# A transformer block in one kernel: a gate tile moves from the attention's filler to the seven-product stage, and the steps around it are set anew

## The chip, the cores and the metric

The kernel runs on one NeuronCore of a Trainium2 chip. The metric is the device time of one execution in microseconds (us); less is better. Engines are named as in the profile: PE (TensorE's matmuls; PEld, its weight loads), DVE (VectorE), ACT (ScalarE), POOL (GpSimd), SP (SyncE, which issues most DMAs).

## The reference

With S = 2048 tokens, width D = 640, 32 heads of 20, a window of W = 256 and a gated layer of Df = 1728:

```python
xn = layernorm(x)
q, k, v = heads(xn @ wqkv)
scores = einsum("bhqd,bhkd->bhqk", q, k) * 20 ** -0.5
mask = (i - j >= 0) & (i - j < 256)
A = einsum("bhqk,bhkd->bhqd", softmax(where(mask, scores, -1e9)), v) @ wo
B = (gelu_tanh(xn @ w_gate) * (xn @ w_up)) @ w_down
return x + A + B
```

Everything is float32. gelu_tanh(g) is 0.5 g (1 + tanh(sqrt(2/pi) (g + 0.044715 g^3))).

## The kernel before

**Precision.** A float32 operand is split into a rounded high part and a low part; a product is three matmuls, high x high, low x high, high x low (`dense_steps`, L104 is its matmul). With 640 = 5 x 128 rows one product of a 128-column weight tile with a chunk of C = 512 tokens is 15 matmuls of 512 columns. There are NC = 4 chunks.

**Stages.** First the layer norm and the first q, k and v products. Then the attention, in units: unit u is a group of four heads (g = u // 4) and a chunk (c = u % 4), 32 in all. Then the pair stage (`gate_up_pair`, matmuls at L893): gate and up products of a tile f for two chunks together, seven products by sums of weights and of tokens in place of eight. Then the output products with `w_down` and `wo` (L1160).

**A unit of attention** has NS = 14 slots, numbered on in `now[0]`. In it lie:
- `max_pair` (matmul L468, DVE L472): scores of 128 queries for two heads, and their masked maximum on DVE; 8 a unit, two at slots 0, 4 and 8 and, from the second unit on, two more at slot 0 behind `av_unit`. They run ahead of the unit that uses them. Their PSUM pool has four banks.
- `exp_piece` (matmul L527, ACT L529): scores and exponentials of one head in one of three banks, two pieces at each of the slots 0, 2, ... 10. The banks are X, Y, Z of `pieces`: X is the diagonal block and the block two back, Y two blocks ahead in the chunk, Z the block one back and one ahead. X and Z read the k of the chunk before. Their PSUM pool (`psx`) has two banks.
- `clear` (POOL L540 and L543) sets masked parts of a finished bank of P to zero, one slot after its last exponential: three clears for X and Y, two for Z (in a first chunk two, three and one).
- `av_unit` (matmul L554) of the unit before, at slot 0; its output takes a bank of `psx` too, which ACT empties (L558).
- `load_stack(u + 3)` at slot 12: twelve DMAs from DRAM on SP's queue, six for q into one of three buffers, six for k into one of four (L447).

**Filler.** Between these, `pull_fill(RATE / NS)` at the end of every slot draws matmuls from a generator, `filler`, which runs the remaining q, k and v products and the gate tiles of `sets`; a matmul counts 1, one of v 0.65. `RATE` is the number a unit. What the attention doesn't draw runs after it. `NFA` is the number of gate tiles in the filler (besides the last, half-wide one): tiles NFA to 12 go to the pair stage. `V1_SLOT` is the slot from which v's second half may be drawn.

**A gate tile in the filler** (`gate_up_fill`) has for each chunk a gate and an up product, each in one of two PSUM banks (`ps_d`), and then five steps on other engines:

```python
c1: gs = copy(gate); t = square(sqrt(0.044715) * gate)      # ACT
c2: t = (t + 1) * gs                                       # DVE L607
c3: t = tanh(sqrt(2 / pi) * t)                             # ACT, LAG slots later
c4: gs = (t + 1) * gs                                      # DVE L615
c5: t = (gs * 0.5) * up                                    # DVE L622, then stored
```

`c5` alone reads the up product, and waits until `c4` has been issued.

**Order.** The order on PE, ACT, DVE and POOL is that in which the Python code issues the instructions. `defer(n, ...)` issues a step n slots later at the slot's start; `late` puts a DVE step behind the maxes and exponentials of its slot (`flush`). `save_qk` uses the same for q and k: a high copy, a difference, and after LAG slots a low copy and a second difference on POOL, then stores.

Of the kernel before, what the change touches and what calls it, by code (L numbers as in the profile page):

```python
# [12 lines left out]
AF = mybir.ActivationFunctionType  # L13
OP = mybir.AluOpType
# [14 lines left out]
SR = 3 * DH  # L29
QROWS = 64 + SR  # L30
NS = 14
RATE = 42.2
V1_SLOT = 158
MXD = 6
LAG = 4
NFA = 6
HD = D // 2
HR = 5
NQD = 9
# [25 lines left out]
def block_kernel(ctx, tc, x, wqk, wv, wgu, wdo, wdl, out):  # L65
    nc = tc.nc
# [17 lines left out]
    qd = [dram.tile([NG, 3, 4 * DH, C], BF, name=f"qd{c}") for c in range(NC)]  # L84
    kd = [dram.tile([NG, 3, 4 * DH, C], BF, name=f"kd{c}") for c in range(NC)]
# [105 lines left out]
    done = set()  # L191
    now = [None]
# [12 lines left out]
    def flush():  # L205
        while lates:
            fn, a = lates.pop(0)
            fn(*a)

    def defer(n, fn, *a):  # L210
        if now[0] is None:
            fn(*a)
        else:
            at(now[0] + n, fn, *a)
# [17 lines left out]
    def save_qk(t, c, ps):  # L232
        pt = qkp.tile([128, 3, C], BF, name="pt", tag="pt")
        r = qkp.tile([128, C], F32, name="r", tag="r", bufs=1)
        dst = (qd if t < 5 else kd)[c]
        h, l = (2, 0) if t < 5 else (0, 2)

        def lower():
            nc.scalar.activation(pt[:, 1, :], r, AF.Copy)  # L239
            nc.gpsimd.tensor_tensor(out=pt[:, l, :], in0=r, in1=pt[:, 1, :], op=OP.subtract)  # L240
            defer(1, store)

        def store():
            a, end = t % 5 * 128, t % 5 * 128 + 128
            while a < end:
                g, b = divmod(a, 4 * DH)
                n = min(4 * DH - b, end - a)
                p = n - end + a + 128
                nc.sync.dma_start(dst[g, :, b:b + n, :].rearrange("p m t -> m p t"), pt[p - n:p])
                a += n  # L250
            done.add((t, c))

        def middle():
            nc.vector.tensor_tensor(out=r, in0=ps, in1=pt[:, h, :], op=OP.subtract)
            defer(1 if now[0] is None or now[0] < NS else LAG, lower)

        def upper():
            nc.scalar.activation(pt[:, h, :], ps, AF.Copy)
            late(middle)

        defer(1, upper)
# [57 lines left out]
    NQ, NK = 3, 4  # L319
    qs = [st1.tile([128, 4, C], BF, name=f"qs{i}") for i in range(NQ)]  # L320
    ks = [st1.tile([128, 4, C], BF, name=f"ks{i}") for i in range(NK)]
# [114 lines left out]
    vtiles = dict(enumerate(v0[2]))  # L436
    ap = pr.enter_context(tc.tile_pool(name="ap", bufs=2, side="right", reuse_waits="tile"))

    def load_stack(u):
        g, c = divmod(u, NC)  # L440
        for m in range(80 * g // 128, (80 * g + 79) // 128 + 1):
            assert (m, c) in done and (m + 5, c) in done, (u, m)

        for dst, src, top, again in ((qs[u % NQ], qd[c], 1, 2), (ks[u % NK], kd[c], 0, 0)):
            for j in (0, 2):
                for p, part, n in ((j * 32, top, 2), (j * 32 + 2 * DH, again, 1), (64 - j * 32, 0, 3)):
                    nc.sync.dma_start(dst[p:p + DH * n, j:j + 2].rearrange("p j t -> p (j t)"),  # L447
                                      src[g, part:part + n].rearrange("s (d j) t -> (s d) (j t)",
                                                                      j=4)[:, j * C:(j + 2) * C])
# [44 lines left out]
    def pieces(c):  # L494
        b = 4 * c
        X = [(b, 0, 0, 384)] + ([(b - 2, 384, 0, 128)] if c else [])
        Y = [(b + 1, 0, 128, 384), (b + 3, 384, 384, 128)]
        Z = ([(b - 1, 0, 0, 256)] if c else []) + [(b + 2, 256, 256, 256)]
        return X, Y, Z

    def diag_tail(kb, col, q0, n, c):
        r = []
# [10 lines left out]
    def exp_piece(u, s):  # L513
        g, c = divmod(u, NC)
        bi, j = divmod(s, 4)
        bank = pieces(c)[bi]
        q = qs[u % NQ]
        if j == 0:
            pts[u, bi] = ap.tile([128, 4, C], F32, name="P", tag="P", bufs=3)
        pt = pts[u, bi]  # L520
        lo = min(p[1] for p in bank)
        hi = max(p[1] + p[3] for p in bank)
        ps = psx.tile([128, C], F32, name="ps_e", tag="ex")
        for kb, col, q0, n in sorted(bank, key=lambda p: p[3]):
            k = ks[(u - (kb < 4 * c)) % NK]
            kc = kb % 4 * 128
            nc.tensor.matmul(ps[:, col:col + n], k[0:QROWS, j, kc:kc + 128], q[0:QROWS, j, q0:q0 + n],  # L527
                             start=True, stop=True)
        nc.scalar.activation(pt[:, j, lo:hi], ps[:, lo:hi], AF.Exp, scale=SCALE)  # L529
        if j == 3:  # L530
            defer(1, clear, u, bi)
# [61 lines left out]
    def gate_up_fill(f, ws, c):  # L593
        cs = slice(c * C, (c + 1) * C)
        pss = []
        st = {}

        def c1():
            gs = st["g"] = hp.tile([128, C], F32, name="gs", tag="gs")
            t = st["t"] = hp.tile([128, C], F32, name="he", tag="he", bufs=2)  # L600
            nc.scalar.activation(gs, pss[0], AF.Copy)
            nc.scalar.activation(t, pss[0], AF.Square, scale=math.sqrt(0.044715))
            defer(1, late, c2)

        def c2():
            gs, t = st["g"], st["t"]
            nc.vector.scalar_tensor_tensor(t, t, 1.0, gs, op0=OP.add, op1=OP.mult)  # L607
            defer(LAG, c3)

        def c3():  # L610
            nc.scalar.activation(st["t"], st["t"], AF.Tanh, scale=math.sqrt(2.0 / math.pi))
            defer(1, late, c4)

        def c4():
            nc.vector.scalar_tensor_tensor(st["g"], st["t"], 1.0, st["g"], op0=OP.add, op1=OP.mult)  # L615
            st["done"] = True

        def c5():
            if "done" not in st:
                defer(1, late, c5)  # L620
                return
            nc.vector.scalar_tensor_tensor(st["t"], st["g"], 0.5, pss[1], op0=OP.mult, op1=OP.mult)  # L622
            defer(1, lambda: nc.sync.dma_start(hd[f][c], st["t"]))

        for i, (wh, wl) in enumerate(ws):
            ps = psd.tile([128, C], F32, name="ps_d", tag="dn")
            pss.append(ps)
            yield from dense_steps(ps, lambda k: wh[:, k, :], lambda k: wl[:, k, :],
                                   lambda k: xh[:, k, cs], lambda k: xl[:, k, cs], KT)
            defer(1, *((late, c5) if i else (c1,)))  # L630

    sets = [("qk", 1), ("gu", 0), ("qk", 2), ("qk", 3), ("qk", 4)]
    sets += [("gu", f) for f in range(1, NFA)] + [("gu", NF - 1)]
    pools = (wp, None), (hp, 2)
    rest = []

    def filler():
# [6 lines left out]
        for s, (kind, i) in enumerate(sets[:-1]):  # L644
            nxt = []
            after = sets[s + 1]
            for c in range(NC):
# [97 lines left out]
    def pull_fill(n):  # L745
        debt[0] += n
        while debt[0] > 0:
            debt[0] -= next(fill, 1.0)

    def attention():  # L750
        now[0] = -1
        load_stack(0)
        load_stack(1)
        load_stack(2)
        for i, (p, k, half) in enumerate((p, k, half) for p in range(NC // 2) for k in range(2) for half in range(2)):
            for j, fn in enumerate(x_sums(p, k, half)):
                at(XS0 + XSN * i + 2 * j, fn)
        for i in range(12):
            now[0] = i - 13
            for fn, a in tick():  # L760
                fn(*a)
            if i % 2 == 0:
                pull_max(2, now[0])
            flush()
            pull_fill(2 * RAMP)
        pull_fill(GAP)
        for u in range(NU + 1):
            for i in range(NS):
                T = now[0] = NS * u + i
                for fn, a in tick():  # L770
                    fn(*a)
                if i in (0, 4, 8) or T == 2:
                    pull_max(2, T)
                if i == 0 and u:
                    av_unit(u - 1)
                    flush()
                    pull_max(2, T)
                if i % 2 == 0 and i < 12 and u < NU:
                    exp_piece(u, i)
                    exp_piece(u, i + 1)  # L780
                flush()
                if i == 12 and 3 <= u + 3 < NU:
                    load_stack(u + 3)
                pull_fill(RATE / NS)
        while acts:
            now[0] += 1
            for fn, a in tick():
                fn(*a)
            flush()
        now[0] = None  # L790
        run(fill)
        assert not acts
# [578 lines left out]
    for n, (p, k) in enumerate(steps):  # L1371
        i = n % (NQD + 1)
# [71 lines left out]
```

## Time and profile before

| | |
|---|---|
| runs, us | 1079.07, 1079.88, 1081.58; median 1079.88 |
| profiled execution: its own time, its span, us | 1078.76, 1076.7 |
| busy share of the span: PE, PEld, DVE, ACT, POOL | 98%, 77%, 69%, 48%, 31% |
| granted PE clock | 1.0 throughout |
| DMA | 158.44 MB, mean 147 GB/s |

Busy shares are means over stages with different limits. A PE matmul is drawn with a modelled end and overlaps the next one, so the distance from start to start is its price in a stream, and a short wait of PE may show no idle time.

### The profile page before, as it was taken

How to read it: one execution, taken by the hardware profiler on the slowest of the kernel's cores; microseconds unless marked ns; L12 is line 12 of the kernel's file. 1: busy time of each engine (PE TensorE's matmuls, PEld its weight loads, DVE VectorE, ACT ScalarE, POOL GpSimd, SP SyncE). 2: the span in 40 equal slices, each digit the busy share in tenths (PEclk: the TensorE clock that was granted, in tenths of full speed). 3: DMA queues.
4: the chain of work that ended last, by engine and by line, in shares of the span. 5: the costliest groups of instructions: out<-in, count | busy, mean ns of one | idle time of the engine just before them, and what ended most of it. 6: DMA issues, size and time to landing. Idle time of an engine off the chain costs nothing.

```text
span 1076.7 us, 21130 instructions
## 1 busy us (share of the span) xinstructions
PE 1055.0 (98%) x7253; PEld 827.3 (77%) x7253; DVE 746.9 (69%) x1985; ACT 516.1 (48%) x1088; POOL 332.6 (31%) x514
## 2 busy tenths in 40 slices
PE   8999999999999999999999999999999999999998
PEld 7977656666678766666666568888888999999998
DVE  7755657666555566776667626788775879888887
ACT  4434655565656565555555465323224544343332
POOL 5022653767554273735446250111100000000000
PEclk9999999999999999999999999999999999999999
DMA  5552343445452244334343226465776873443343
GB/s 202 181 160 67 100 142 114 132 142 175 132 157 75 87 124 146 116 109 132 96 121 113 70 63 198 160 239 199 262 232 242 276 261 126 127 126 119 123 135 103
DMA packets 105170, 158.44 MB, mean 147 GB/s; under 512 B 15420, under 2 KB 60092, under 8 KB 105064
## 3 DMA queue, kind: packets, MB, share of 16 engines
q1 hardware_dynamic: 102680, 150.95, 44.4%
q10 hardware_dynamic: 2384, 6.16, 1.8%
q8 instruction: 57, 0.93, 0.4%
q14 instruction: 49, 0.40, 0.1%
HBM read 101.78 MB, written 54.92 MB: 146 GB/s over the span
## 4 chain that ended last, share of the span: by engine, by line
PE 79%; DVE 8%; DMA 4%; POOL 3%; issue 3%; ACT 2%; SPq 1%; ACTq 0%; DVEq 0%; POOLq 0%
PE ps_d L104 23%; PE ps L1160 16%; PE ps_g L893 15%; PE ps_e L527 7%; PE ps_v L104 6%; PE ps_o L554 6%; PE ps_m L468 4%; DVE junk L472 2%; PE ps_g L104 1%; POOL pt L240 1%; DVE ss L998 1%; DVE at L998 1%; DMA hr<-od 1%; PE ps_t L179 1%; DMA qs<-qd 1%
## 5 line engine op out<-in xcount | busy, mean ns | idle before, releaser
L472 DVE CUSTOM_DVE_ANT_0 junk<-ps_m,mask 128x384 bf16<-128x384 f32 (+2 forms) x512 | 272.2, 532 | 157.1 <-PE ps_m L468 99.2
L529 ACT ACTIVATE P<-ps_e 128x512 f32<-128x512 f32 (+2 forms) x384 | 198.4, 570 | 93.3 <-PE ps_e L527 85.2
L1160 PE MATMUL ps<-wb,at 128*128 128x320 f32 x999 | 156.8, 309 | 1.0 <-DVE at L998 0.9
L1160 PEld LDWEIGHTS ps<-wb,at 128*128 128x128 f32 x999 | 148.9, 188 | 2.1 <-DVE at L998 1.4
L540 POOL TENSOR_SCALAR_AFFINE_SELECT P<-P 128x512 f32<-128x512 f32 x128 | 84.2, 658 | 178.7 <-ACT P L529 178.5
L104 PE MATMUL ps_d<-xh,wqh 128*128 128x512 f32 x430 | 127.2, 409 | 3.3 <-DVE he L622 3.3
L104 PE MATMUL ps_d<-xh,wql 128*128 128x512 f32 x430 | 126.8, 408 | 0.0
L104 PE MATMUL ps_d<-xl,wqh 128*128 128x512 f32 x430 | 126.4, 406 | 0.0
L527 PE MATMUL ps_e<-qs,ks 124*128 124x128 bf16 (+2 forms) x704 | 114.6, 277 | 1.5 <-ACT P L529 0.9
L527 PEld LDWEIGHTS <-ks 124*128 124x128 bf16 x704 | 49.8, 98 | 58.9 <-issue 48.7
L104 PEld LDWEIGHTS ps_d<-xh,wqh 128*128 128x128 f32 x430 | 78.3, 189 | 21.3 <-DVE he L622 6.3
L104 PEld LDWEIGHTS ps_d<-xl,wqh 128*128 128x128 f32 x430 | 79.2, 189 | 15.7 <-issue 1.7
L104 PEld LDWEIGHTS ps_d<-xh,wql 128*128 128x128 f32 x430 | 79.0, 189 | 14.4 <-issue 0.5
L1160 PE MATMUL ps<-wt,at 128*128 128x320 f32 x552 | 89.2, 310 | 0.8 <-DVE xr L1183 0.8
L554 PE MATMUL ps_o<-P,v 128*32 128x384 f32 (+2 forms) x1408 | 84.5, 386 | 0.0
L1160 PEld LDWEIGHTS ps<-wt,at 128*128 128x128 f32 x552 | 82.9, 188 | 1.3 <-DVE xr L1183 1.0
L1114 ACT ACTIVATE at<-ss 128x512 fp32r<-128x512 f32 x59 | 37.3, 632 | 91.1 <-DVE ss L998 91.1
L543 POOL TENSOR_SCALAR_AFFINE_SELECT P<-P 128x512 f32<-128x512 f32 x112 | 70.5, 640 | 26.5 <-ACT P L529 26.2
L240 POOL TENSOR_TENSOR pt<-r,pt 128x512 bf16<-128x512 f32 x40 | 46.6, 1164 | 96.3 <-ACT pt L239 85.1
L468 PE MATMUL ps_m<-ks,qs 60*128 60x128 bf16 (+1 forms) x704 | 67.6, 275 | 6.5 <-DVE mx L472 2.4
L558 ACT ACTIVATE ob<-ps_o 128x512 f32<-128x512 f32 x32 | 19.1, 597 | 112.5 <-PE ps_o L554 101.9
L554 PEld LDWEIGHTS ps_o<-P,v 128*32 128x32 f32 x1408 | 40.1, 110 | 34.5 <-issue 25.1
(189 smaller groups left out, 1677.1 us busy)
## 6 DMA issues: line engine op xcount, KB each, us to landing
hr<-hd SPq DMA_DIRECT2D x104, 128.0 KB
hd<-he SPq DMA_DIRECT2D x50, 256.0 KB
wr<-wgu SPq DMA_DIRECT2D x27, 320.0 KB
qs<-qd SPq DMA_DIRECT2D x64, 120.0 KB
ks<-kd SPq DMA_DIRECT2D x64, 120.0 KB
xi<-x SPq DMA_DIRECT2D x16, 320.0 KB
qs<-qd SPq DMA_DIRECT2D x64, 80.0 KB
ks<-kd SPq DMA_DIRECT2D x64, 80.0 KB
```

What stands on the lines that cost most here:

```text
L104: nc.tensor.matmul(ps, a(k), b(k), start=n == 0, stop=n == 3 * nk - 1)
L240: nc.gpsimd.tensor_tensor(out=pt[:, l, :], in0=r, in1=pt[:, 1, :], op=OP.subtract)
L468: nc.tensor.matmul(ps[:, lo:hi], q[rows, j, 128 * b:128 * b + 128], kt[rows, j, k0:k1], start=True, stop=True, tile_position=(64 * r, 0))
L472: nc.vector.tensor_tensor_reduce(out=junk[:, 0:n], in0=ps[:, 0:n], in1=mask[:, 384 - n:384], scale=1.0, scalar=NEG, op0=OP.add, op1=OP.max ...
L527: nc.tensor.matmul(ps[:, col:col + n], k[0:QROWS, j, kc:kc + 128], q[0:QROWS, j, q0:q0 + n], start=True, stop=True)
L529: nc.scalar.activation(pt[:, j, lo:hi], ps[:, lo:hi], AF.Exp, scale=SCALE)
L540: nc.gpsimd.affine_select(out=a, in_=a, pattern=[[0, 4], [1, 128]], compare_op=OP.is_ge, fill=0.0, base=0, channel_multiplier=-1)
L543: nc.gpsimd.affine_select(out=a, in_=a, pattern=[[0, 4], [-1, 128]], compare_op=OP.is_ge, fill=0.0, base=-1, channel_multiplier=1)
L554: nc.tensor.matmul(o[32 * j:32 * j + 32, q0:q0 + n], v[:, w0_:w0_ + 32], pt[:, j, col:col + n], start=i == 0, stop=i == len(todo) - 1, ski ...
L893: nc.tensor.matmul(ps, i, j, start=first and n == 0, stop=n == len(work) - 1, skip_group_check=True)
L1114: nc.scalar.activation(hi[:, 3:7], s, AF.Copy)
L1160: nc.tensor.matmul(ps[bank][:, 0:HD], *work[bank][j], start=bank not in begun, stop=final[p, bank] == n and j == len(work[bank]) - 1, skip ...
```

## The change

- A sixth gate tile, number 5, leaves the filler (NFA from 6 to 5) and goes through `gate_up_pair`, in seven products. RATE falls from 42.2 to 38.4 a unit, and V1_SLOT moves from 158 to 170.
- The gate's steps are taken in another order: half the gate is kept, the up product is multiplied into it (c4) as soon as it is there, and the product with 1 + tanh comes last (c5). c5 waits until the tanh has been issued.
- LAG becomes a table by slot within the unit, of 1 to 5 slots.
- `load_stack` issues the six DMAs of k at slot 9; those of q stay at slot 12.
- The three banks of a unit are taken in the order X, Z, Y.
- At slot 0, from the second unit on, one filler step stands between the two exponential pieces; the slot's own share is lessened by it.

```diff
-RATE = 42.2
-V1_SLOT = 158
+RATE = 38.4
+V1_SLOT = 170
-LAG = 4
-NFA = 6
+KSLOT = 9
+LAG = 3, 5, 4, 4, 4, 4, 3, 3, 4, 3, 2, 1, 1, 1
+NFA = 5
...
+    def lag():
+        return 1 if now[0] is None or now[0] < NS else LAG[now[0] % NS]
...
-            defer(1 if now[0] is None or now[0] < NS else LAG, lower)
+            defer(lag(), lower)
...
-    def load_stack(u):
+    def load_stack(u, which=(0, 1)):
...
-        for dst, src, top, again in ((qs[u % NQ], qd[c], 1, 2), (ks[u % NK], kd[c], 0, 0)):
+        for i in which:
+            dst, src, top, again = ((qs[u % NQ], qd[c], 1, 2), (ks[u % NK], kd[c], 0, 0))[i]
...
-        return X, Y, Z
+        return X, Z, Y
...
-            nc.scalar.activation(gs, pss[0], AF.Copy)
+            nc.scalar.activation(gs, pss[0], AF.Copy, scale=0.5)
...
-            defer(LAG, c3)
+            defer(lag(), c3)
 
         def c3():
-            nc.scalar.activation(st["t"], st["t"], AF.Tanh, scale=math.sqrt(2.0 / math.pi))
-            defer(1, late, c4)
+            nc.scalar.activation(st["t"], st["t"], AF.Tanh, scale=2.0 * math.sqrt(2.0 / math.pi))
+            st["tanh"] = now[0]
 
         def c4():
-            nc.vector.scalar_tensor_tensor(st["g"], st["t"], 1.0, st["g"], op0=OP.add, op1=OP.mult)
-            st["done"] = True
+            nc.vector.tensor_tensor(out=st["g"], in0=pss[1], in1=st["g"], op=OP.mult)
+            defer(1, late, c5)
 
         def c5():
-            if "done" not in st:
+            if now[0] is not None and st.get("tanh", now[0]) >= now[0]:
                 defer(1, late, c5)
                 return
-            nc.vector.scalar_tensor_tensor(st["t"], st["g"], 0.5, pss[1], op0=OP.mult, op1=OP.mult)
+            nc.vector.scalar_tensor_tensor(st["t"], st["t"], 1.0, st["g"], op0=OP.add, op1=OP.mult)
             defer(1, lambda: nc.sync.dma_start(hd[f][c], st["t"]))
...
-            defer(1, *((late, c5) if i else (c1,)))
+            defer(1, *((late, c4) if i else (c1,)))
...
                     exp_piece(u, i)
+                    if i == 0 and u:
+                        pull_fill(1)
+                        debt[0] -= 1
                     exp_piece(u, i + 1)
                 flush()
-                if i == 12 and 3 <= u + 3 < NU:
-                    load_stack(u + 3)
+                if u + 3 < NU and i in (KSLOT, 12):
+                    load_stack(u + 3, (int(i == KSLOT),))
                 pull_fill(RATE / NS)
```

More of the change, by code (lines that the diff above doesn't have):

```diff
@@ L437, in block_kernel @@
     ap = pr.enter_context(tc.tile_pool(name="ap", bufs=2, side="right", reuse_waits="tile"))
-    def load_stack(u):
+    def load_stack(u, which=(0, 1)):
         g, c = divmod(u, NC)
         for m in range(80 * g // 128, (80 * g + 79) // 128 + 1):
-            assert (m, c) in done and (m + 5, c) in done, (u, m)
-        for dst, src, top, again in ((qs[u % NQ], qd[c], 1, 2), (ks[u % NK], kd[c], 0, 0)):
+            assert all((m + 5 * i, c) in done for i in which), (u, m)
+        for i in which:
+            dst, src, top, again = ((qs[u % NQ], qd[c], 1, 2), (ks[u % NK], kd[c], 0, 0))[i]
             for j in (0, 2):
```

## The prediction

> **What bounds the kernel now.** I read the page's head first, then busy time by stage, then the waits of PE, then single stretches of the timeline where those waits lie.
>
> ```profile
> span 1076.7 us, 21130 instructions
> PE 1055.0 (98%) x7253; PEld 827.3 (77%) x7253; DVE 746.9 (69%) x1985; ACT 516.1 (48%) x1088; POOL 332.6 (31%) x514
> PE   8999999999999999999999999999999999999998
> ...
> PEclk9999999999999999999999999999999999999999
> ```
>
> PE is busy from end to end and its clock is granted in full, so a microsecond of PE work that goes is a microsecond of time, unless a wait takes its place. The next view gives busy time by stage, cut at the first attention-times-v unit (107.74), the last one (644.77), the first of the seven-product pairs (661.5) and their end (833); below them stands one steady unit of attention.
>
> ```profile
> core 0: us, PE busy (x) PEld busy (x) DVE busy (x) ACT busy (x) POOL busy (x), PEclk, DMA share, GB/s
> ...
> 107.74:644.77 537.03, 527.38 (x4117) 349.90 (x4115) 335.46 (x1104) 305.52 (x652) 280.88 (x453) 1.00 0.39 118
> 644.77:661.50 16.73, 16.73 (x111) 12.93 (x110) 10.09 (x17) 8.77 (x14) 2.50 (x2) 1.00 0.51 155
> 661.50:833.00 171.50, 171.50 (x758) 141.98 (x757) 127.29 (x212) 55.50 (x102) 17.91 (x12) 1.00 0.65 222
> ...
> 473.79:490.75 16.96, 16.96 (x134) 11.06 (x132) 11.94 (x40) 10.52 (x20) 7.69 (x14) 1.00 0.34 103
> ```
>
> The pair stage has no idle PE time at all, the attention 537.03 - 527.38 = 9.65 us in 31 units. What made up those 9.65 us is in PE's waits:
>
> ```profile
> PE ps_d L104 <- DVE he L622: 3.3, 6, 0.9
> ...
> PE ps_m L468 <- DVE mx L472: 2.4, 7, 0.4
> PE ps_m L468 <- DMA ks<-kd: 2.2, 3, 1.3
> ...
> PE ps_e L527 <- ACT P L529: 0.9, 1, 0.9
> ...
> PE ps_e L527 <- ACT ob L558: 0.4, 1, 0.4
> ```
>
> **The change, part by part: the sixth tile.** In the filler a gate tile is 2 x 15 matmuls of 512 columns in each of four chunks, 120. As seven products it is 6 + 9 + 6 + 9 + 6 + 9 + 9 = 54 for a pair of chunks, 108 for two. The price of one is the distance from start to start, not the duration shown:
>
> ```profile
> L893 PE MATMUL ps_g<-xh,wqh x126: 389/389/390, 661.5 to 832.2; 128*128 128x512 f32 x126
> ...
> L893 PE MATMUL ps_g<-xl,wqh x126: 389/389/390, 662.4 to 832.7; 128*128 128x512 f32 x126
> ...
> 488.33 1.31 PE L104 MATMUL ps_d<-xh,wqh 128*128 128x512 f32 x5
> 489.48 1.07 PE L104 MATMUL ps_d<-xh,wql 128*128 128x512 f32 x4
> ```
>
> Seven pairs of loops, 14 x 54 = 756 matmuls, start between 661.5 and 832.7: (832.7 - 661.5) / 755 = 0.227 us each, though each lasts 0.389; five in the attention take 1.15 us, 0.230 each. So attention loses 120 x 0.227 = 27.2 us of PE work, the pair stage gains 108 x 0.227 = 24.5, net **-2.7 us**. The Trainium skill, page "TensorE: Matmul & The Clock Gate", section "Back-to-back issue gap", gives 131 ns for such a matmul in a sustained stream (216 isolated); by that the term would be 12 x 0.131 = 1.6 us, and no stretch here comes near 131 ns.
>
> What the tile brings besides lies beside that PE work: its weight sums and additions go to DVE, which is busy 127.29 of 171.5 us there, its splits to ACT (55.50) and POOL (17.91). The new pair is one more round of a loop that runs without a gap, and the first round is prepared, as before, under the 60 matmuls of the last tile. I take zero. If that cover failed, the pairs would wait once for their splits and sums, at most the 60 x 0.227 = 13.6 us that it lasts.
>
> The unit's 42.2 steps become 38.4, so a unit of 16.96 us becomes 16.96 - 3.8 x 0.227 = 16.1. Since filler and slots shrink together, the filler still ends in the last unit; nothing is left over at either end.
>
> **Up ahead of the tanh.** Here is where the first wait comes from. A group of 15 matmuls needs the PSUM bank that holds an up product, and that is released only by the last DVE step, which waits for tanh and sits behind the maxes:
>
> ```profile
> 593.18 1.43 PE L104 MATMUL ps_d<-xh,wqh 128*128 128x512 f32 x5 [0.87 <-DVE he L622]
> ...
> L615 DVE SCALAR_TENSOR_TENSOR gs<-he,gs 128x512 f32<-128x512 f32 x24 | 16.7, 695 | 19.7 <-ACT he L611 19.7
> L622 DVE SCALAR_TENSOR_TENSOR he<-gs,ps_d 128x512 f32<-128x512 f32 x24 | 16.5, 687 | 1.6
> ```
>
> The new order reads the bank one slot after the up product, with no tanh ahead of it; still three DVE operations of about 0.7 us a chunk, so DVE's load doesn't change. Even behind four maxes it is through before the 15 matmuls of the next gate have run (15 x 0.227 = 3.4 us, plus attention's own). The six waits go: 3.3 us shown, and since a matmul is drawn 0.389 long while the next could start after 0.227, each shown gap hides 0.16 more: 3.3 + 6 x 0.16 = **-4.3 us** (bounds -4.3 and 0).
>
> The table of lags moves tanh and the low parts of q and k within their slots. They are the same ACT operations, off the path; a lag of 1 stands only for slots 11 to 13, where no exponentials follow. Too short a lag would park ACT, and behind it the exponentials, on DVE; that is in the term for new waits.
>
> **k stack at slot 9.** Twelve DMAs were issued at slot 12, k after q. They, and the maxes that need them:
>
> ```profile
> 142.94 2.19 SPq L447 DMA_DIRECT2D qs<-qd  x6
> 145.18 2.20 SPq L447 DMA_DIRECT2D ks<-kd  x6
> ...
> 150.09 0.21 PE L468 MATMUL ps_m<-ks,qs 60*128 60x128 bf16 x1 [1.33 <-DMA ks<-kd]
> 150.79 0.49 PE L468 MATMUL ps_m<-ks,qs 60*128 60x128 bf16 x7 [0.48 <-DMA ks<-kd]
> ```
>
> All six k transfers stand behind q's 2.2 us of issue. With k three slots (about 3.4 us) earlier, q alone is last, 2.2 us earlier than k was; the waits were 1.33 + 0.48 here and 0.42 elsewhere: **-2.2 us** (0 if q's landing takes their place). The k rows are free by then because the older keys' products now come second in the unit (X, Z, Y). SP waits at slot 9 for the last of them; behind it stand only stores and q, with three slots of room.
>
> **One step between the first two exponentials.** At slot 0 the second exponential's scores need the bank that ACT is just emptying of attention's output:
>
> ```profile
> 476.52 0.50 PE L468 MATMUL ps_m<-ks,qs 60*128 60x384 bf16 x4
> 476.95 0.73 PE L527 MATMUL ps_e<-qs,ks 124*128 124x128 bf16 x4
> 477.38 0.99 PE L104 MATMUL ps_d<-xl,wqh 128*128 128x512 f32 x3
> ...
> 478.89 0.61 PE L527 MATMUL ps_e<-qs,ks 124*128 124x128 bf16 x4
> 479.21 0.54 PE L104 MATMUL ps_d<-xh,wqh 128*128 128x512 f32 x1
> ...
> 458.90 0.93 PE L468 MATMUL ps_m<-ks,qs 60*128 60x384 bf16 x4
> 459.76 0.61 PE L527 MATMUL ps_e<-qs,ks 124*128 124x128 bf16 x4
> 460.07 1.46 PE L104 MATMUL ps_d<-xh,wqh 128*128 128x512 f32 x5
> ```
>
> From the scores to the next filler step it is 0.43 us at slot 0 and 0.32 at slot 2: 0.11 us lost, though no idle time is printed. Where the maxes ahead were held (458.90 to 459.76, 0.86 instead of 0.43), as after the eight short units, the bank is free and it is 0.31. A step of 0.227 in between covers 0.11: 24 x 0.10 = **-2.4 us** (bounds 31 x 0.11 = -3.4 and, if switching to the step and back costs 0.02, +0.6).
>
> **The new order's clears.** Y has three mask clears where Z had two, and Y now comes last before attention times v:
>
> ```profile
> 471.70 0.64 POOL L543 TENSOR_SCALAR_AFFINE_SELECT P<-P 128x512 f32<-128x512 f32 x1 [2.45 <-ACT P L529]
> 472.29 0.64 POOL L540 TENSOR_SCALAR_AFFINE_SELECT P<-P 128x512 f32<-128x512 f32 x1
> ...
> 405.39 2.80 PE L554 MATMUL ps_o<-P,v 128*32 128x384 f32 x48
> 405.48 0.64 POOL L540 TENSOR_SCALAR_AFFINE_SELECT P<-P 128x512 f32<-128x512 f32 x1
> ```
>
> In the quiet unit the last clear ends at 472.93, 0.86 us ahead of the product at 473.79; a third (0.59 apart) would end 0.27 ahead, and the third bank is not read until over half of the 2.8 us product. But where POOL also has sums of x and weights to do, the last clear ends 0.73 us into the product (406.12), and a third would end at 1.3, with a short unit (two banks of few blocks ahead) getting two more. I charge **+2 us** for a few such units (0, and 31 x 0.6 = 19 if every unit were so late).
>
> **Denser slots.** Each maximum costs DVE more than its busy time:
>
> ```profile
> 577.50 0.56 DVE L472 CUSTOM_DVE_ANT_0 junk<-ps_m,mask 128x384 bf16<-128x384 f32 x1
> ...
> 578.21 0.56 DVE L472 CUSTOM_DVE_ANT_0 junk<-ps_m,mask 128x384 bf16<-128x384 f32 x1
> ...
> 270.55 0.32 PE L468 MATMUL ps_m<-ks,qs 60*128 60x384 bf16 x1 [0.39 <-DVE mx L472]
> ```
>
> One takes 0.71 us from start to start, 16 of them 11.4 us a unit. A unit holds 42.2 / 30 = 1.4 chunks of three operations at 0.7: 2.9; together 14.3 of 16.96, 84%. After: 11.4 + 38.4 / 30 x 2.1 = 14.1 of 16.1, 88%. A wait on a maximum is 0.39 us shown, 0.55 with what is hidden; there are seven now. I charge four more, **+2 us** (0, and two a unit, 31 x 1.1 = 34).
>
> **Sum.** -2.7 - 4.3 - 2.2 - 2.4 + 2 + 2 = -7.6 us. The profiled execution took 1078.76 us (span 1076.7 and 2.1 around it) and would take 1071.2; the median of the runs, 1079.88, lies 1.1 above it, so I forecast 1079.9 - 7.6 = **1072.3**.
>
> **Rivals.** *Nothing new waits*: all four gains and no charge, -11.6: 1068.3. For it: the maxes' queue holds only earlier maxes ahead of what PE needs. Against: 88%. Chance 0.16.
>
> *Only the products count*: each removed wait is taken over by another (q's landing for k's, DVE's queue for tanh): -2.7, 1077.2. Chance 0.17.
>
> *Slower: DVE becomes the unit's bound.* PE reaches the second maxes of slot 0 and those of slot 8 before DVE has emptied the banks, in every unit. Two waits of 0.39 in 24 units: 18.7 us, against -9.6 (the four gains and the +2 for clears): 1079.9 + 9.1 = 1089. It decides from 9.6 / 31 = 0.31 us a unit, less than one wait. For it: 0.71 against 0.56 busy; against: the steady unit above has no gap at all, and filler takes its DVE work with it. Chance 0.10.
>
> *Attention isn't held by PE.* Its chain of maximum, exponential and clear holds the unit at 16.96, and the 120 matmuls leave without shortening it: +24.5 for the pair stage, -8.9 for the three waits: 1095. Against it: 16.96 busy of 16.96. The Trainium skill, page "Perfetto Trace Analysis", section "Identifying the Most-Contended Engine", calls matmul busy share a bad measure of PE's headroom and wants the share of weight loads; here that is 349.90 of 537.03, 65%, in attention and 83% in the pairs, which speaks for this rival; the start-to-start distance of 0.23 us in both stages speaks against it. Chance 0.03.
>
> *The late clears eat it*: 0.3 us in most units: +9 in place of +2, so -0.6, 1079.3. Chance 0.04.
>
> **How the numbers follow.** The forecast has the remaining 0.50; its own range, with either charge between 0 and 4 us, is 1068 to 1076. The range of 1067 to 1078.5 takes in the first two rivals and leaves out the last three, 0.17, and little at the low end. This measurement can tell 0.2%, 2.2 us. Faster: 0.50 + 0.16 + 0.12 of the second rival, whose -2.7 is just outside: 0.78. Same: its other 0.05 and the clears' 0.04: 0.09. Slower: 0.13.
>
> **What would show it.** Right: pairs 24.5 us longer at 0.227 a matmul and without gaps; from the first to the last attention-times-v unit about 31 x 0.86 = 27 us less and some 6 us more; no wait on the gate's DVE steps or on k in PE's waits; 0.32 instead of 0.43 at slot 0. Wrong: waits on maxima of more than 10 us, weight loads of attention times v waiting on POOL, exponentials waiting for ACT behind a tanh, or a unit that stays near 16.9.

## The result and the profile after

The changed kernel takes 1066.47 us, median of four runs (1065.18 to 1067.78), the kernel before beside it 1080.22: ratio 0.9872, 95% interval 0.9855 to 0.9889. That is 13.8 us less, where 7.6 were forecast, and 0.5 us below the forecast range.

The head of the page of the changed kernel, then its busy time by the same stages as before: first to last attention-times-v unit, the last half-wide tile, the pairs (up to 820), the output products.

```profile
span 1064.9 us, 21151 instructions
PE 1048.8 (98%) x7241; PEld 825.2 (77%) x7241; DVE 751.4 (71%) x1996; ACT 516.2 (48%) x1088; POOL 335.5 (32%) x506
```

```profile
core 0: us, PE busy (x) PEld busy (x) DVE busy (x) ACT busy (x) POOL busy (x), PEclk, DMA share, GB/s
0.00:108.80 108.80, 101.44 (x656) 85.95 (x656) 69.60 (x212) 46.19 (x140) 31.32 (x48) 0.98 0.47 151
108.80:606.38 497.58, 495.41 (x3998) 326.92 (x3997) 325.21 (x1092) 299.37 (x640) 279.85 (x441) 1.00 0.42 123
606.38:622.90 16.52, 16.52 (x110) 12.80 (x110) 10.48 (x17) 8.47 (x14) 3.44 (x4) 1.00 0.49 153
622.90:820.00 197.10, 197.10 (x872) 163.30 (x871) 141.34 (x236) 63.05 (x117) 20.89 (x14) 1.00 0.59 203
820.00:1064.90 244.90, 238.30 (x1613) 236.24 (x1611) 204.72 (x441) 99.09 (x179) 0.00 (x0) 1.00 0.48 155
```

The attention went from 537.03 to 497.58 us, **39.4 less**. Its idle PE time, as drawn, went from 9.65 to 497.58 - 495.41 = 2.17 us. Two of the seven waits on maxima that the prediction shows lie ahead of the attention. Within it PE waited 16 times before (he 3.3 us, ks 2.2, maxima 1.7, ACT's P 0.9, ob 0.4), and he and ks are gone now. The line on maxima before, then all of PE's waits after, both within the attention:

```profile
PE ps_m L468 <- DVE mx L472: 1.7, 5, 0.4
```

```profile
PE ps_e L532 <- ACT P L534: 0.5, 1, 0.5
PE ps_m L473 <- DVE mx L477: 0.3, 1, 0.3
PE ps_e L532 <- ACT ob L563: 0.2, 1, 0.2
```

The pairs, by first and last start of two of their groups:

```profile
L901 PE MATMUL ps_g<-xh,wqh x144: 389/389/389, 623.6 to 818.8; 128*128 128x512 f32 x144
...
L901 PE MATMUL ps_g<-xl,wqh x144: 389/389/389, 624.5 to 819.2; 128*128 128x512 f32 x144
```

16 x 54 = 864 matmuls start within 195.6 us, 0.227 apart, and the stage is 197.10 of 197.10 busy. From the first matmul of the last half-wide tile to the first output product it is 185.07 us before and 209.53 after: 24.46 more, against the 24.5 forecast. Ahead of that tile three filler steps are left over where there was one, 0.45 us: the filler no longer quite ends in the last unit.

So the attention's 39.4 us are 120 x 0.227 = 27.2 us of matmuls and, by difference, **12.2 us of waits**, of which 9.65 - 2.17 = 7.5 had been drawn as idle and 4.7 had not. The forecast had 8.9 for waits, less 4 for new ones.

Two stages without a change scatter from run to run: up to the first attention-times-v unit it is 106.5 to 110.5 us in the profiles of this study, and the output products take 242.0 to 245.5. The attention repeats far better: 497.58 us here, 497.62 in the second profile of the same kernel (after_again). Below, the attention's length stands for a kernel, from the start of its first `av_unit` to that of its last, read from the timeline; the pairs add 24.5 a tile. There is one profile behind each length, and every edit also moves work against the slots. Drawing v's second half 12 slots later, with no other change, moved the attention by 0.1 us in one kernel (before_v170) and by 3.1 in another (tile_v182 against tile_alone). So a difference of one or two microseconds between two kernels need not be the edit's own price.

### The profile page after: what moved, and what is told of

It reads as the page before. It is cut to its first block, busy times and chain, and to the rows that moved or that the text cites. A ratio compares the mean times of both kernels' runs of the same rounds, so it can differ in the third digit from the quotient of the medians.

```text
span 1064.9 us, 21151 instructions
## 1 busy us (share of the span) xinstructions
PE 1048.8 (98%) x7241; PEld 825.2 (77%) x7241; DVE 751.4 (71%) x1996; ACT 516.2 (48%) x1088; POOL 335.5 (32%) x506
## 4 chain that ended last, share of the span: by engine, by line
PE 85%; DVE 8%; DMA 2%; ACT 2%; issue 2%; POOL 1%; SPq 0%; ACTq 0%; DVEq 0%; POOLq 0%
PE ps_d L105 25%; PE ps_g L901 17%; PE ps L1168 16%; PE ps_e L532 8%; PE ps_v L105 6%; PE ps_o L559 6%; PE ps_m L473 5%; DVE junk L477 2%; PE ps_g L105 1%; DMA stg<-wtd 1%; DVE at L1006 1%; DVE ss L1006 1%; DVE wb L1006 1%; DVE wt L1006 1%; PE ps_t L180 1%
## 5 line engine op out<-in xcount | busy, mean ns | idle before, releaser
L545 POOL TENSOR_SCALAR_AFFINE_SELECT P<-P 128x512 f32<-128x512 f32 x128 | 84.9, 663 | 166.3 <-ACT P L534 164.3
L105 PE MATMUL ps_d<-xh,wqh 128*128 128x512 f32 x390 | 119.0, 415 | 0.0
L105 PE MATMUL ps_d<-xh,wql 128*128 128x512 f32 x390 | 118.7, 415 | 0.0
L105 PE MATMUL ps_d<-xl,wqh 128*128 128x512 f32 x390 | 118.4, 412 | 0.0
L532 PE MATMUL ps_e<-qs,ks 124*128 124x128 bf16 (+2 forms) x704 | 117.5, 278 | 0.9 <-ACT P L534 0.5
L105 PEld LDWEIGHTS ps_d<-xh,wqh 128*128 128x128 f32 x390 | 71.8, 190 | 13.4 <-ACT xh L188 1.4
L105 PEld LDWEIGHTS ps_d<-xh,wql 128*128 128x128 f32 x390 | 72.4, 191 | 12.3
L105 PEld LDWEIGHTS ps_d<-xl,wqh 128*128 128x128 f32 x390 | 71.6, 189 | 13.0 <-issue 0.8
L548 POOL TENSOR_SCALAR_AFFINE_SELECT P<-P 128x512 f32<-128x512 f32 x112 | 72.2, 655 | 23.4 <-ACT P L534 23.4
L244 POOL TENSOR_TENSOR pt<-r,pt 128x512 bf16<-128x512 f32 x40 | 46.7, 1167 | 76.4 <-ACT pt L243 68.1
```

The lines of the kernel that those rows point to most:

```text
L105: nc.tensor.matmul(ps, a(k), b(k), start=n == 0, stop=n == 3 * nk - 1)
L545: nc.gpsimd.affine_select(out=a, in_=a, pattern=[[0, 4], [1, 128]], compare_op=OP.is_ge, fill=0.0, base=0, channel_multiplier=-1)
L548: nc.gpsimd.affine_select(out=a, in_=a, pattern=[[0, 4], [-1, 128]], compare_op=OP.is_ge, fill=0.0, base=-1, channel_multiplier=1)
```

## The experiments

Each ratio is to the kernel before on the same chip.

| kernel | ratio to before (95%) | attention, us |
|---|---|---|
| before | 1 | 537.0 |
| changed kernel | 0.9872 (0.9855 to 0.9889) | 497.6 |
| tile_alone | 0.9951 (0.9934 to 0.9968) | 506.7 |
| order_alone | 0.9954 (0.9939 to 0.9969) | 531.6 |
| kslot_alone | 0.9976 (0.9963 to 0.9989) | 533.4 |
| step_alone | 0.9974 (0.9959 to 0.9989) | 534.0 |
| six_tiles | 0.9914 (0.9889 to 0.9939) | 525.9 |
| without_order | 0.9875 (0.9857 to 0.9893) | 498.4 |
| without_kslot | 0.9872 (0.9853 to 0.9892) | 497.9 |
| without_step | 0.9892 (0.9876 to 0.9908) | 499.5 |
| lag_four | 0.9892 (0.9868 to 0.9916) | 499.7 |
| before_v170 | 0.9986 (0.9971 to 1.0001) | 537.2 |
| before_rate | 1.0002 (0.9986 to 1.0019) | 536.0 |
| tile_v182 | 0.9932 (0.9912 to 0.9952) | 503.6 |
| four_tiles | 0.9859 (0.9834 to 0.9884) | 473.2 |
| three_tiles | 0.9874 (0.9849 to 0.9899) | 451.7 |
| sums_early | 0.9878 (0.9859 to 0.9897) | 475.1 |
| four_xyz | 0.9950 (0.9935 to 0.9965) | 484.0 |
| four_late | 0.9822 (0.9795 to 0.9849) | 470.5 |
| after_again | 0.9859 (0.9834 to 0.9884) | 497.6 |

The ratios can't tell without_order, without_kslot, without_step, lag_four, four_tiles, three_tiles or sums_early from the changed kernel; for these only the lengths of the attention speak. In sums_early and in four_xyz the attention holds one stretch of 3.41 us at half clock each (last section).

### One part at a time, in the kernel before

**The tile alone.**

```diff
-RATE = 42.2
-V1_SLOT = 158
+RATE = 38.4
+V1_SLOT = 170
-NFA = 6
+NFA = 5
```

> The kernel before with the sixth tile alone moved (NFA 5, RATE 38.4, V1_SLOT 170); steps of the gate, lags, stacks and banks as before. Theory 'PE holds it, denser slots cost nothing': 12 matmuls less, -2.7 us, and PE's waits in the attention stay about as before (he 3.3, mx 2.4, ks 2.2 us). Rival 'denser slots cost': waits of PE on maxima and on the gate's DVE steps grow by over 2 us, the time falls by less than 1 us or rises.

Neither theory: 0.9951 is 5.3 us, twice the 2.7. The attention fell by 30.4 us, 3.1 more than its matmuls, and the pairs rose by 24.46. PE's waits of the whole run:

```profile
PE ps_m L468 <- DMA ks<-kd: 3.3, 5, 0.9
...
PE ps_m L468 <- DVE mx L472: 1.5, 4, 0.5
...
PE ps_d L104 <- DVE he L622: 1.0, 2, 0.6
```

With the gate's old steps the wait on he fell from 3.3 to 1.0 us, and the maxima's from 2.4 to 1.5. Those on DMAs grew, from 2.2 to 5.3 with two smaller lines. Together the drawn idle time of the attention fell by only 1.3 us; where the other 1.8 lay isn't shown.

**The order of the gate's steps alone.** As in the diff of the change, with `defer(LAG, c3)` kept.

> The kernel before with the gate's new order of steps alone (up times half the gate ahead of 1 + tanh), lag 4 as before. Theory 'bank only': the waits of PE on he go, -4.3 us, the waits on maxima stay (2.4 us). Rival 'DVE no longer parked on tanh': the waits on maxima shrink as well, to about 1 us, and the time falls by 6 us or more. Rival 'returned': a new wait on gs or the bank, no change.

5.0 us by the ratio, 5.45 in the attention; the line on he is gone and that on maxima is not smaller:

```profile
PE ps_m L468 <- DVE mx L472: 2.9, 8, 0.5
...
PE ps_e L527 <- ACT P L529: 1.5, 1, 1.5
...
PE ps_m L468 <- DMA ks<-kd: 0.4, 1, 0.4
```

That is the theory of the bank, with 4.3 us for it. The wait on ks at unit 3 went as well, from 1.8 to 0.6 us (now put down to a store, td<-tx), though no stack was moved, and the waits on maxima and on ACT's P grew by 0.5 and 0.6. So about 1 us of the 5.45 stays unexplained.

**k's stack at slot 9, banks X, Z, Y.**

```diff
-        return X, Y, Z
+        return X, Z, Y
...
-                if i == 12 and 3 <= u + 3 < NU:
-                    load_stack(u + 3)
+                if u + 3 < NU and i in (9, 12):
+                    load_stack(u + 3, (int(i == 9),))
```

> The kernel before with k's six DMAs at slot 9 and the banks in the order X, Z, Y, nothing else. Theory 'k was last': the waits on ks (2.2 us shown) go, -2.2 to -2.9 us, and no weight load of attention times v waits longer on POOL. Rival 'clears': Y's third clear holds PE in units where POOL is busy, +2 us or more, so about no change. Rival 'q takes its place': a wait on qs<-qd of the same size.

2.6 us by the ratio, 3.6 in the attention. No ks and no qs line is left, and he and the maxima are as before (3.3 and 2.3); the one wait of an exponential on ACT, 0.9, went too. Y's third clear held nothing.

**One step between two exponentials.**

```diff
                     exp_piece(u, i)
+                    if i == 0 and u:
+                        pull_fill(1)
+                        debt[0] -= 1
                     exp_piece(u, i + 1)
```

> The kernel before with one filler step between the first two exponential pieces of slot 0, nothing else. Theory 'covers the bank': the 0.11 us between scores and next step at slot 0 goes in 24 to 31 units, -2.4 to -3.4 us. Rival 'switching costs as much': between -0.6 and +0.6 us.

2.8 us by the ratio, 3.0 in the attention, as the first theory has it; 0.8 of it is again the wait on ks, 2.2 us and now 0.5, with 0.9 put down to td<-tx. The longer unit that the prediction shows at 476.95, in the changed kernel (scores, the step, scores, filler):

```profile
450.01 0.39 PE L532 MATMUL ps_e<-qs,ks 124*128 124x128 bf16 x2
450.11 0.53 PE L105 MATMUL ps_d<-xh,wqh 128*128 128x512 f32 x1
450.48 0.40 PE L532 MATMUL ps_e<-qs,ks 124*128 124x128 bf16 x2
450.58 0.53 PE L105 MATMUL ps_d<-xh,wqh 128*128 128x512 f32 x1
450.94 1.08 PE L105 MATMUL ps_d<-xh,wql 128*128 128x512 f32 x4
```

Four scores and two steps take 450.94 - 450.01 = 0.93 us, with a third step 1.16. Before, four scores and three steps took 478.21 - 476.95 = 1.26: the 0.10 us of the forecast. In the eight units behind a short one nothing is gained, as the prediction has it. In the other 23 the same stretch is shorter by about 0.10 us in eleven, by 0.15 in seven (the short units themselves), by 0.23 in one, and hardly in four. The sum over the units falls by 2.1 us in step_alone, and by 2.2 from without_step to the changed kernel: mechanism and size of the forecast hold.

### One part taken out of the changed kernel

Alone, the four parts bring 5.4, 5.3, 3.6 and 3.1 us of attention, last tile and pairs together (725.17 us before), 17.4 in sum; the changed kernel has 14.5. The next runs take one out at a time.

```diff
six_tiles:
-RATE = 38.4
-V1_SLOT = 170
-NFA = 5
+RATE = 42.2
+V1_SLOT = 158
+NFA = 6
without_order: c1, c3, c4, c5 as in the kernel before, with defer(lag(), c3)
without_kslot:
-        return X, Z, Y
+        return X, Y, Z
-                if u + 3 < NU and i in (KSLOT, 12):
-                    load_stack(u + 3, (int(i == KSLOT),))
+                if u + 3 < NU and i == 12:
+                    load_stack(u + 3)
without_step:
-                    if i == 0 and u:
-                        pull_fill(1)
-                        debt[0] -= 1
lag_four:
-LAG = 3, 5, 4, 4, 4, 4, 3, 3, 4, 3, 2, 1, 1, 1
+LAG = (4,) * 14
```

> The changed kernel without the moved tile: NFA 6, RATE 42.2, V1_SLOT 158. Theory 'the terms add': 2.7 us slower than the changed kernel, about 1069, attention 27 us longer and the rest 24.5 shorter. Rival 'the tile brings more, by how its steps fall on the slots': 5 us slower, as the tile alone brought 5, with waits on he or on maxima that the changed kernel lacks.

> The changed kernel with the gate's old order of steps (tanh ahead of the up product), table of lags kept. Theory 'the terms add': 5 us slower than the changed kernel, as the order alone brought 5. Rival 'overlap': at 38.4 steps a unit the gate's groups fall elsewhere on the slots and the waits on he are few anyway (the tile alone had 1.0 us of them): 1 to 2 us slower.

> The changed kernel with all twelve stack DMAs at slot 12 and the banks in the order X, Y, Z. Theory 'the terms add': 3 to 4 us slower, waits on ks of 2 us or more in PE's list. Rival 'overlap': the new phases dodge the late stacks, under 1 us slower.

> The changed kernel without the filler step between the first two exponential pieces. Theory 'the terms add': 2 to 3 us slower, 0.11 us more at slot 0 of every longer unit. Rival: no change, since other waits take the time up.

> The changed kernel with a lag of 4 at every slot in place of the table. Theory 'off the path': within 1 us of the changed kernel, the same waits. Rival 'the table keeps DVE from waiting on tanh, or ACT from coming late to an exponential': waits on maxima or on ACT's P grow by over 1 us, +1 to +4 us.

Taken out, the tile costs 3.5 us of attention and pairs (28.3 less 24.3 and a little at the seam), the order 0.8, k's slot with the banks 0.3, the step 1.9, the table of lags 2.1: 8.6 in sum, less than the 14.5. So the parts **overlap**: the order and k's slot each bring what another part would bring as well. (None of the five differences but the tile's is above the 3.1 us that a move of v's second half alone brought.) The old order of steps at 38.4 filler steps has hardly a wait on he (first line, without_order); the new order at 42.2 has none, but longer waits on maxima (second, six_tiles); and with stacks at slot 12 and the banks X, Y, Z the wait on ks is 0.5 where it was 2.2 (third, without_kslot).

```profile
PE ps_d L105 <- DVE he L627: 0.4, 1, 0.4
```

```profile
PE ps_m L473 <- DVE mx L477: 3.1, 9, 0.5
```

```profile
PE ps_m L473 <- DMA ks<-kd: 0.5, 1, 0.5
```

lag_four shows a wait on q's stack that the changed kernel lacks, 0.9, and over the whole run 1.8 on maxima for 1.1: against the prediction's nothing, the table may be worth up to 2.1 us here. It wasn't tried in the kernel before.

### Phase, or slots to a group

Three runs were to move the phase of the filler against the slots and leave the work as it is.

```diff
before_v170 (kernel before):
-V1_SLOT = 158
+V1_SLOT = 170
before_rate (kernel before):
-RATE = 42.2
+RATE = 42.6
tile_v182 (tile_alone):
-V1_SLOT = 170
+V1_SLOT = 182
```

> The kernel before with V1_SLOT 170 alone: v's second half is drawn 12 slots later, so the groups of the gate tiles behind it fall on other slots, and no work changes. Theory 'phase': the waits on he and ks, 5.5 us shown, come out differently by 2 us or more, and the time with them (1074 to 1082). Rival 'the order makes the waits': 5 to 6 us shown, the time as before.

> The kernel before with RATE 42.6 alone, one per cent more filler a slot. Theory 'phase': the waits on he and ks (5.5 us shown) change by 2 us or more either way. Rival 'the order makes the waits': within 1 us of 5.5.

> The kernel of the run tile_alone with V1_SLOT 182 in place of 170. Theory 'phase': what the tile alone brought beyond the 2.7 us of its matmuls came from where its groups fell on the slots, so the waits shown in the attention (8 us there, 1.0 of them on he) change by 2 us or more. Rival 'the tile itself': the same 5.3 us, the same waits.

For he only before_rate is such a test. With another V1_SLOT every gate group (24 and 20 of them) stays at its place within its unit, to a hundredth of a unit, and he waits in the same units as before; the equal readings of before_v170 and tile_v182 say nothing of phase. In before_rate the twenty groups behind unit 17 lie elsewhere, he waits in four units in place of six, and it is 3.1 us for 3.3: near this rate one other phase changed little. First before_v170, then before_rate, then tile_v182:

```profile
PE ps_d L104 <- DVE he L622: 3.3, 6, 0.9
```

```profile
PE ps_d L104 <- DVE he L622: 3.1, 4, 1.1
```

```profile
PE ps_d L104 <- DVE he L622: 1.0, 2, 0.6
```

For ks phase does matter: 2.0, 0.8 and 1.8 us, with 2.2 in the kernel before and 3.3 in tile_alone; and in tile_v182 the attention is 3.1 us shorter than in tile_alone for nothing but v's second half drawn later.

What sets he may then be the filler's rate. A gate's chain is laid out in slots: the step that frees the up product's bank is issued a fixed number of slots after the gate's group. Until the group that wants the bank, the up product and the next gate have to run, 15 filler steps each, and 15 steps are 15 / (42.2 / 14) = 5.0 slots before and 15 / (38.4 / 14) = 5.5 after. Thinner filler gives the chain half a slot more for each group. This arithmetic fits the readings of he with the old order (3.1 to 3.3 at 42.2 to 42.6; 1.0, 1.0, 0.4 at 38.4), but it is argued and not shown: the rate was moved together with the tile, at 38.4 the groups lay at one set of places only, and no run changed the slots of the chain by themselves.

The waits on maxima go the same way. Within the attention they are 0.9 to 2.4 us in the seven kernels at 42.2 or 42.6 and 0 to 0.9 in the seven at 38.4. Part of it is phase: V1_SLOT alone took them from 1.7 to 0.9 (before_v170). Why they fall with thinner filler isn't shown.

### How far the exchange carries, and a version that beats both

> The changed kernel with one tile more in the pair stage: NFA 4, RATE 34.7, the first gate tile behind the third q and k tile (so that q and k are ready in time). A unit is 15.2 us by PE, DVE's maxima and gate steps 13.8 of it, 91%. Theory 'PE holds it': 12 matmuls less again, -2.7 us against the changed kernel, 1063.8. Rival 'denser slots cost': the waits on maxima grow from 1.1 to over 4 us and the time doesn't fall.

> The changed kernel with NFA 3, RATE 31.0 and the first gate tile behind all q and k tiles. A unit is 14.4 us by PE, DVE's share of it 94%. Theory 'PE holds it': -5.4 us against the changed kernel, 1061. Rival 'denser slots cost': waits on maxima and of exponentials on ACT of over 8 us in the attention, the time equal to the changed kernel's or above.

For both, q and k have to be ready in time:

```diff
-RATE = 38.4
-NFA = 5
+RATE = 34.7
+NFA = 4
-    sets = [("qk", 1), ("gu", 0), ("qk", 2), ("qk", 3), ("qk", 4)]
+    sets = [("qk", 1), ("qk", 2), ("qk", 3), ("gu", 0), ("qk", 4)]
```

(three_tiles: RATE 31.0, NFA 3, `("gu", 0)` last.) The fourth tile takes 24.4 us off the attention, the third 21.4, where 27.2 would have paid for the pairs' 24.5 and 2.7 more; the time is level. At four tiles the missing 2.8 us are mostly this, three times over; POOL's row first, then PE's, in four_tiles:

```profile
247.23 1.17 POOL L244 TENSOR_TENSOR pt<-r,pt 128x512 bf16<-128x512 f32 x1
248.35 0.75 POOL L690 TENSOR_TENSOR tx<-tx,xl 128x256 f32<-128x256 f32 x1
249.04 0.89 POOL L593 TENSOR_TENSOR wql<-wr,wqh 128x128 fp32r<-128x128 f32 x2
249.88 0.64 POOL L545 TENSOR_SCALAR_AFFINE_SELECT P<-P 128x512 f32<-128x512 f32 x1
250.47 0.64 POOL L548 TENSOR_SCALAR_AFFINE_SELECT P<-P 128x512 f32<-128x512 f32 x1
251.05 0.64 POOL L545 TENSOR_SCALAR_AFFINE_SELECT P<-P 128x512 f32<-128x512 f32 x1
```

```profile
248.18 1.93 PE L559 MATMUL ps_o<-P,v 128*32 128x384 f32 x32
251.16 1.07 PE L559 MATMUL ps_o<-P,v 128*32 128x384 f32 x16 [1.05 <-POOL P L548]
```

The product of attention and v stands at its third bank until the second of POOL's clears of it ends at 251.11, because sums of x (L690), weight splits (L593) and a low part of q or k (L244) were queued ahead; the third clear, still running then, held nothing. Clears that come too late, as the prediction charged them, are met one tile later. Three runs ask what to do about it.

```diff
sums_early (four_tiles):
-                at(XS0 + XSN * i + 2 * j, fn)
+                at(28 + 14 * (2 * i + j // 5) + 2 * (j % 5), fn)
four_late (four_tiles):
-                at(XS0 + XSN * i + 2 * j, fn)
+                at(14 * (14 + 2 * i + j // 5) + 2 * (j % 5), fn)
four_xyz (four_tiles): banks and stacks as in without_kslot
```

> Four tiles as in the run four_tiles, with POOL's sums of x put at slots 0 to 8 of units 2 to 17, five a unit, in place of every second slot of stretches of 20 slots. Theory 'late clears': three units of four_tiles lost 2.0 us to clears behind these sums; they go, the attention is 2 us shorter and the time about 1062, below both kernels. Rival 'the lost time is elsewhere, in DVE's maxima': as four_tiles, 1064.

sums_early: the waits on clears fell from 1.4 to 0.3 us, but two waits on q's stack, 2.2 in sum, came instead, and the attention is 1.9 us longer, not 2 shorter. Up to 1.7 of these 1.9 us are clock: behind the two waits PE's granted clock is 0.50 for 3.41 us (the last row), at most half of it lost. Half a theory.

```profile
225.10 0.23 PE L473 MATMUL ps_m<-ks,qs 60*128 60x128 bf16 x1 [1.66 <-DMA qs<-qd]
225.87 0.80 PE L473 MATMUL ps_m<-ks,qs 60*128 60x128 bf16 x7 [0.54 <-DMA qs<-qd]
```

```profile
225.46:228.87 3.41, 3.00 (x14) 2.12 (x14) 2.14 (x7) 1.18 (x3) 0.96 (x2) 0.50 0.55 166
```

> Four tiles as in the run four_tiles, with the banks back in the order X, Y, Z and all stack DMAs at slot 12. Theory 'late clears': the 1.4 us of waits on POOL's clears, 2.0 with what is hidden, go; k at slot 12 costs 0.3 us, as in without_kslot; about 1062, below the changed kernel. Rival 'k has to be early at this density': waits on ks of 2 us or more come back, 1064 or above.

four_xyz refutes my reading that the third clear is to blame: with two clears in the last bank the waits on POOL are the same three, and the attention is 10.8 us longer than in four_tiles, 7.7 of it drawn as waits on ks, qd and kd, and up to 1.7 by one more stretch at half clock behind two of these waits.

```profile
PE ps_m L473 <- DMA ks<-kd: 5.2, 7, 1.5
PE ps_m L473 <- DMA qd<-pt: 1.5, 1, 1.5
PE ps_o L559 <- POOL P L548: 1.4, 3, 1.0
...
PE ps_m L473 <- DMA kd<-pt: 1.0, 1, 1.0
```

So POOL's backlog is the cause, not Y's clears, as four_late below bears out; and k's slot with the order of banks, 0.3 us at five tiles, is some nine at four (one phase was tried).

> Four tiles as in the run four_tiles, with POOL's sums of x at slots 0 to 8 of units 14 to 29, behind the q, k and v work of the filler. Theory 'POOL's backlog': the waits on clears (1.4 us shown, 2.0 with what is hidden) came of those sums beside the splits and q and k steps, and neither they nor the wait on q's stack of sums_early (2.2) is there: attention 2 us shorter than in four_tiles, about 1062, 2 us or more below the changed kernel on the same chip. Rival: as four_tiles, level with the changed kernel.

> The changed kernel once more, beside four_late on the same chip: 0.987 of the kernel before, attention 497.6 us, pairs 209.5.

With the sums of x behind the filler's q, k and v work, four_late takes 1060.38 us (1058.49 to 1061.56), the changed kernel on the same chip 1063.81 (1062.71 to 1067.01), the kernel before 1080.60: 0.9822 (0.9795 to 0.9849). The slowest run of four_late is below the fastest of the changed kernel. Its attention is 27.1 us shorter than the changed kernel's, all of the 27.2, and PE's waits within it are these two:

```profile
PE ps_m L473 <- DVE mx L477: 0.4, 1, 0.4
PE ps_e L532 <- ACT ob L563: 0.2, 1, 0.2
```

## Why the prediction was wrong

The direction, the bound and the three waits were right; the two charges for new waits failed, one of them in its sign. Of the rivals, *nothing new waits* (-11.6 us, chance 0.16) came nearest to the 13.8 us measured.

- *Twelve matmuls at 0.227, -2.7*: right, at both ends. The pairs grew by 24.46 for 24.5 without a gap. The 131 ns of the Trainium skill (page "TensorE: Matmul & The Clock Gate", section "Back-to-back issue gap") were met in no stretch. That nothing is left over at either end was off by two filler steps, 0.45 us.
- *PE holds the attention*: right, against the rival drawn from the share of weight loads. PEld was 349.90 of 537.03, 65%, and is 326.92 of 497.58, 66%, while the stage lost the matmuls' whole 27.2 us. On the page "Perfetto Trace Analysis" of the Trainium skill (section "Identifying the Most-Contended Engine") this trace differs: the share of weight loads was no measure of PE's room here, the distance between starts was.
- *Denser slots, +2*: **the step that failed**, in its sign. I had DVE's share of a unit (84% to 88%) and charged four more waits on maxima. Within the attention they fell from five to one, 1.7 to 0.3 us, and with 0.16 us hidden at each that is 2.1 us gained for 2 charged. In the 14 kernels above they are smaller at 38.4 steps a unit than at 42.2, so a fuller DVE didn't mean more waits. What makes them fall stays open: part of it is phase, and slots per group is an argument for he and not for maxima. More waits on maxima come only later (three_tiles, 2.6 us of them within the attention, where the third tile brought 21.4 of 27.2).
- *The new order's clears, +2*: **failed too**, measured 0. The unit whose clears ended 0.86 us before its product now has them end at 446.81, 0.04 before 446.85, as the rows below show (the second is the first half of the product); the third bank is read over a microsecond later, and no product waited. Weight loads of these products wait for POOL about as often as before, 27 times and now 25, 0.4 us at the longest in both. The backlog I feared cost some 2 us at four tiles, and there for POOL's queue, not for the third clear.

```profile
446.17 0.64 POOL L545 TENSOR_SCALAR_AFFINE_SELECT P<-P 128x512 f32<-128x512 f32 x1
...
446.85 1.50 PE L559 MATMUL ps_o<-P,v 128*32 128x384 f32 x24
```

- *The three waits, -4.3 - 2.2 - 2.4*: about right. By the same rule, the idle time drawn and 0.16 us hidden at each gap, he is 3.3 + 6 x 0.16 = 4.3 us and ks 2.2 + 3 x 0.16 = 2.7; the step brought 2.1. That is 9.1 for 8.9, an estimate. Each edit alone brought more in the attention (5.45, 3.6 and 3.0 us), since it shifted other waits as well, and they don't add: he goes by the order or with the moved tile, and ks was made smaller by kslot_alone, order_alone, step_alone and before_rate.
- *The table of lags, 0*: up to 2.1 us in the changed kernel, not told apart from phase.

The forecast's sum was -7.6. Of the 12.2 us of waits, 9.1 are the three forecast ones, 2.1 the maxima and 0.4 ACT's P, 11.6 in sum; 0.6 isn't accounted for. Without the two charges and with the waits at their measured 12.2 for 8.9 the sum would have been -14.9, against 14.5 measured in attention, last tile and pairs; the rest is the two filler steps left over.

## What to carry to other kernels

Where one engine is the bound and its work is interleaved by hand in slots, don't charge new waits from busy shares alone: here DVE's busy share of the attention rose from 62% to 65% and the waits on it fell. Count a dependent chain also in slots against the slots its neighbours take. The idle time drawn for a pipelined engine is a lower bound; starts compared unit by unit, with and without an edit, show what isn't drawn. Make sure that a run meant to move a phase moves the groups in question: V1_SLOT left them where they were. And measure parts both alone and taken out, since several edits may each remove the same wait; an edit that looks worthless in one kernel (k's slot with the banks, 0.3 us) can hold up the next step (some nine, at one tile less in the filler).

## What the runs showed of the hardware

PE's clock falls to half for 3.41 us after a short gap, in some executions only. Both kernels wait 1.04 us for DVE at 62.7 us. The kernel before goes on at 0.23 us a matmul there (its clock is 1.0 from 5.9 us on); the changed kernel's profile shows eight matmuls 0.43 us apart, and a granted clock of 0.50 (last row, columns as in the view by stage):

```profile
62.74 0.27 PE L473 MATMUL ps_m<-ks,qs 60*128 60x256 bf16 x1 [1.04 <-DVE xl L189]
62.94 2.22 PE L105 MATMUL ps_d<-xh,wqh 128*128 128x512 f32 x5
64.95 2.13 PE L105 MATMUL ps_d<-xh,wql 128*128 128x512 f32 x5
66.92 1.32 PE L105 MATMUL ps_d<-xl,wqh 128*128 128x512 f32 x5
```

```profile
63.29:66.70 3.41, 3.41 (x10) 2.63 (x9) 1.36 (x8) 0.00 (x0) 0.00 (x0) 0.50 0.79 233
```

Ten starts take 66.92 - 62.94 = 3.98 us, where the kernel before takes 65.28 - 62.88 = 2.40: 1.6 us lost. The Trainium skill, page "TensorE: Matmul & The Clock Gate", Part 1, tells of a free-running window of 3413 ns and of a fall to half clock after an idle window. The length agrees; that a gap of 1.04 us was enough differs from the idle window of about 3.4 us in its table.

Where the windows lie tells the executions apart. In each of the 20 profiled ones the clock first rises 4.1 to 7.1 us after the start, and every later stretch at half clock begins a whole number of windows of 3.413 us after that rise; the one above begins (63.29 - 5.26) / 3.413 = 17.0 windows after it. All 20 have the gap of 1.04 us, and in eleven the clock falls behind it: those in which the next window begins 0.5 to 1.0 us after the gap's end. In the other nine it begins within 0.2 us of that end, or 1.25 us and more after it. The two stretches within an attention (sums_early, 64 windows after the rise, and four_xyz, 42) each follow two DMA waits of 2.2 us in sum. What a window counts isn't shown.
